# Linear attention into two expert networks on one core: q's softmax subtraction and exponential issued one slot sooner

## Chip, cores and metric

One core of a Trainium2 chip runs the whole kernel. The metric is the device time of one execution in microseconds (us); the median of three runs of the kernel before is 1250.62 us.

## What is computed

The inputs are q, k and v of shape (8 batches, 8 heads, 576 tokens, 64). The reference, cut to what matters:

```python
q_s = softmax(q, axis=-1)            # over the 64 features of a token
k_s = softmax(k, axis=2)             # over the 576 tokens
kv = einsum('bhsd,bhse->bhde', k_s, v)
x = einsum('bhsd,bhde->bhse', q_s, kv)        # then (4608 tokens, 512)
e = argmax(x @ w_gate)               # one of 8 experts per token
y = gate * sigmoid(x @ w_output_gate)[e] * (relu(x @ w1[e]) @ w2[e])
out = max(y @ m1, y @ m2, y @ m3) @ m_out
```

## The kernel before, in words

The kernel has an attention phase that runs beside the experts' matrix products, and then a second network with the products of `m_l1` and `m_l2`. All matrix products of the experts use operands that are split into an upper and a lower part (three products for one), so each product needs two helpers: ScalarE (ACT) writes the upper part, VectorE (DVE) or GpSimd (POOL) the lower part as a difference.

The first phase is written out by hand in **slots**. A slot is one group of 12 expert products (`l1_group`, L604, or `l2_group`, L622), followed by the reading out of its sum from PSUM, and then by the attention steps that were registered for that slot with `at` (L497). `run_events` (L548) issues them in the order in which they were registered; instructions are issued to each engine in exactly this program order, and every engine works its queue in order. A batch has 32 slots, in four blocks of eight groups: `l1`, `l2`, `l1`, `l2`. The `l1` groups and the first block of `l2` are read out by ACT (L616, L634). The second block of `l2` is read out by DVE (L636).

A **unit** is half of a batch's heads, so there are 16 units, n = 0 to 15. Units 0 and 1 run ahead of the experts. Units 2 and 3 have tables of their own (`EARLY`). For n from 4 on the steps stand at `START[n] = 16 n - 51` plus the offsets in `STEADY` (L44): the front steps (`q_max`, `q_exp`, `k_max`, `k_tr`, `k_exp`, `q_sum`, `kv_mm`, `kv_norm`, `kv_lo`, `q_norm`) and, for each of the two pairs of heads, the back steps (`q_tr`, `q_lo`, `x_mm`, `x_lo`, `logit_mm`). One unit starts every 16 slots, so the back steps of the unit before lie beside the front steps of the next one. Around slot START[n] - 2 to START[n] + 1 these are, in the order in which they are registered (steps of unit n-1 come first in a slot):

- slot START - 2: `x_lo` of pair 0 of unit n-1 (DVE, L371); odd slot, so `split_lo` of the experts' weights on POOL (L595)
- slot START - 1: `logit_mm` of pair 0, then `q_tr` of pair 1 of unit n-1 (five transposes on TensorE into PSUM, copied by ACT, L327), then `q_exp` of unit n, then `split_sub` of the experts' weights on ACT (L588)
- slot START: `q_lo` of pair 1 of unit n-1 (DVE, L335, needs the copy of L327), then `k_tr` of unit n (transposes, then DVE L238 and L241)
- slot START + 1: `x_mm` of pair 1 of unit n-1 (six products, L353, need the result of L335), then `k_exp` of unit n (product L248, needs L241; then DVE L251, ACT L253)

`q_exp` (L224) is two instructions on one tile in place: the subtraction of the row maximum on DVE (L228, 128x1280, both inputs in SBUF) and the exponential on ACT (L229). It issues no DMA.

```python
    def q_exp(b, hb):
        u = units[b, hb]
        qt = u["q"].rearrange("p h c d -> p (h c) d")
        eng = nc.gpsimd if (b, hb) == (0, 1) else vec
        eng.tensor_tensor(out=qt, in0=qt, in1=u["qm"].to_broadcast([128, 20, D]), op=ALU.subtract)
        act(out=qt, in_=qt, func=ACTF.Exp)
```

For odd n the slots around START lie in the second block of `l2` (fh = 1, read out by DVE L636), and the router of the batch before still scatters its token table with indirect DMAs from POOL (`route_5`, L489). For even n they lie in the first block of `l2` (fh = 0, read out by ACT L634). On POOL the decoding of the second network's weights also runs there (L685, L686, L695).

Of the kernel before, what the change touches and what calls it, by code (L numbers as in the profile page):

```python
# [16 lines left out]
PSUM = bass.MemoryType.PSUM  # L17
# [11 lines left out]
CAP = 96  # L29
SLOT = 64  # L30
# [4 lines left out]

# batches whose attention output comes from plain float32 products instead of three with split operands
NFULL = 2

# The order of the work beside the experts' matrix products, in slots of one group of 12 products; a unit is
# half of a batch's heads. STEADY: slots after a unit's START for the steps in FRONT, and those in BACK for  # L40
# each pair of heads; EARLY: the same for the first units, from the first slot on. LOAD: a unit's loads.
# ROUTE: the router's steps after START of a batch's second unit, for batch 0 and 1 from the first slot on.
# DEC: pieces of the float64 weights, after START of even units, of odd units and of the last one.
STEADY = ((-4, -1, -4, 0, 1, 3, 6, 6, 7, 8), (10, 10, 13, 14, 15), (15, 16, 17, 18, 19))  # L44
EARLY = {
# [11 lines left out]
def tile_linear_attention__then__moe(  # L57
# [21 lines left out]

# [1 line left out]
    const = ctx.enter_context(tc.tile_pool(name="const", bufs=1))  # L81
# [24 lines left out]

# [1 line left out]
    es_moe = ExitStack()  # L108
# [20 lines left out]

# [1 line left out]
    def setup():  # L131
# [40 lines left out]

# [1 line left out]
    units = {}  # L174
# [197 lines left out]

    # the logits with tokens as columns: column tile c of the array takes tokens 128 c on; the last 64 follow on tile 0
    def logit_mm(b, hb, pr):
# [17 lines left out]

# [1 line left out]
    def route_1(b):  # L394
# [60 lines left out]
    def route_4(b):  # L455
        pool = nc.gpsimd
        r = rt[b]
        oh, cs, nm = r["oh"], r["cs"], r["nm"]
        cb = cbuf[b % 2]
        for c in range(4):  # L460
            pool.tensor_tensor(out=cb[:, c + 1], in0=cb[:, c], in1=cs[:, 0, c], op=ALU.add)
        n_b = n_all[:, E * b:E * b + E]
        s_b = st_all[:, E * b:E * b + E]
        pool.tensor_tensor(out=n_b, in0=r["cnt"], in1=nm[:, 0], op=ALU.mult)
        pool.tensor_copy(pad_a[:, 4:12], n_b)
        pool.tensor_tensor(out=pad_b[:, 4:12], in0=pad_a[:, 4:12], in1=pad_a[:, 3:11], op=ALU.add)
        pool.tensor_tensor(out=pad_a[:, 4:12], in0=pad_b[:, 4:12], in1=pad_b[:, 2:10], op=ALU.add)
        pool.tensor_tensor(out=pad_b[:, 4:12], in0=pad_a[:, 4:12], in1=pad_a[:, 0:8], op=ALU.add)
        pool.tensor_tensor(out=s_b, in0=pad_b[:, 4:12], in1=n_b, op=ALU.subtract)
        pool.tensor_tensor(out=s_b, in0=s_b, in1=base.to_broadcast([128, E]), op=ALU.add)  # L470
        pool.tensor_tensor(out=base, in0=base, in1=pad_b[:, 11:12], op=ALU.add)
        mo = sm.tile([128, 5, E], F32, tag="rmo", name="rmo")
        pool.tensor_tensor(out=mo, in0=oh, in1=nm.to_broadcast([128, 5, E]), op=ALU.mult)
        a = sm.tile([128, 5, E], F32, tag="ra", name="ra")
        pool.tensor_tensor(out=a, in0=cs[:, 1], in1=cb[:, 0:5], op=ALU.add)
        pool.tensor_tensor(
            out=a, in0=a, in1=s_b.rearrange("p (o e) -> p o e", o=1).to_broadcast([128, 5, E]), op=ALU.add
        )
        # the position of a token that leaves its batch's majority expert; BIG for the others
        pool.tensor_scalar(out=a, in0=a, scalar1=-float(BIG), scalar2=None, op0=ALU.add)  # L480
        pool.tensor_tensor(out=a, in0=a, in1=mo, op=ALU.mult)
        for w in (4, 2, 1):
            pool.tensor_tensor(out=a[:, :, 0:w], in0=a[:, :, 0:w], in1=a[:, :, w:2 * w], op=ALU.add)
        pi = sm.tile([128, 5], I32, tag="rpi", name="rpi")
        pool.tensor_scalar(out=pi, in0=a[:, :, 0], scalar1=float(BIG), scalar2=None, op0=ALU.add)
        r["pi"] = pi
# [6 lines left out]

# [1 line left out]
    events = {}  # L495
# [55 lines left out]

# [1 line left out]
    raw_t = {}  # L553
# [98 lines left out]

# [1 line left out]
    dec = deque((i, j) for j in range(8) for i in range(4))  # L654
# [12 lines left out]
    def dec_bits():  # L667
        if not dec_r:
            return
        i, j, raw = dec_r.popleft()  # L670
        lo, hi = raw[:, :, 0], raw[:, :, 1]
        f = dc_p.tile([128, 384], I32, tag="df", name="df")
        p = dc_p.tile([128, 384], I32, tag="dp", name="dp")
        a2 = dc_p.tile([128, 384], F32, tag="da", name="da")
        r = dc_p.tile([128, 384], F32, tag="dr", bufs=2, name="dr")
        # sign, exponent less 896 and the upper 20 bits of the mantissa
        vec.tensor_scalar(out=f, in0=hi, scalar1=0x07FFFFFF, scalar2=3,
                          op0=ALU.bitwise_and, op1=ALU.logical_shift_left)
        vec.scalar_tensor_tensor(out=f, in0=hi, scalar=-0x40000000, in1=f,
                                 op0=ALU.bitwise_and, op1=ALU.bitwise_or)  # L680
        vec.tensor_scalar(out=p, in0=f, scalar1=-0x00800000, scalar2=None, op0=ALU.bitwise_and)
        act(out=a2, in_=hi.bitcast(F32), func=ACTF.Abs)
        # the lower 32 bits, added with one rounding
        act(out=r, in_=lo.bitcast(U32), func=ACTF.Copy, scale=2.0 ** -52)
        nc.gpsimd.tensor_tensor(out=r, in0=r, in1=p.bitcast(F32), op=ALU.mult)  # L685
        nc.gpsimd.tensor_tensor(out=r, in0=r, in1=f.bitcast(F32), op=ALU.add)  # L686
        dec_m.append((i, j, a2, r))

    def dec_store():
        if not dec_m:  # L690
            return
        i, j, a2, r = dec_m.popleft()
        # under float32's range, by the upper word (0x38100000 and on, read as a float): zero
        vec.tensor_scalar(out=a2, in0=a2, scalar1=1.125 * 2.0 ** -15, scalar2=None, op0=ALU.is_ge)
# [9 lines left out]

# [1 line left out]
    m_all = [t.rearrange("p j n -> (p j n)").rearrange("(k f) -> k f", f=F2) for t in w32_d[0:3]]  # L706
# [29 lines left out]

    # ================= program =================
    with tc.manual_schedule():
# [95 lines left out]

# [1 line left out]
        sl = {}  # L836

        def fx_table():
# [43 lines left out]
            vec.tensor_reduce(out=sf[:, 0:4], in_=pr, axis=AX.X, op=ALU.add)  # L882
            # start = valid * (start0 + SLOT * j)
            vec.tensor_scalar(out=sf[:, 4:5], in0=jc, scalar1=float(SLOT), scalar2=None, op0=ALU.mult)
            vec.scalar_tensor_tensor(
                out=sf[:, 2:3], in0=sf[:, 4:5], scalar=sf[:, 3:4], in1=sf[:, 2:3], op0=ALU.mult, op1=ALU.add
            )
            # static start = min(start + CAP * (1 - valid), CAP)
            vec.tensor_scalar(
# [3 lines left out]
            vec.tensor_scalar(out=sf[:, 3:4], in0=sf[:, 4:5], scalar1=float(CAP), scalar2=None, op0=ALU.min)  # L893
            # trips of the general loop: 0 where the static slots cover everything
            nsl = incl[:, w - 1:w]
# [55 lines left out]

        # half a piece of a minority expert's weights: 256 rows of 512 columns
        def fx_w(e_reg, i):
# [33 lines left out]

        # the tokens' upper and lower parts side by side: the first pass multiplies both with the
        # weights' upper part, the second the upper part with the weights' lower part
        def fx_mm(ps, x, ws, kh):  # L990
# [9 lines left out]

        # adds the two parts and turns tokens to columns
        def fx_sum(raw):
# [62 lines left out]

        # steps between the groups of the second network; one that leaves its sum open in PSUM comes
        # only where the next step follows before that bank is needed again
        fix = deque((f, False) for f in (fx_table, fx_gather, fx_soft, lambda: None, fx_tr))
# [12 lines left out]

        # chunks: (sources of y, N, list of (scale, writer))
        def chunk_l2(c, hs, part=0):
# [20 lines left out]

        # chunk B holds the last 64 tokens of each batch, in two parts; the second carries the packed tokens
        order = [(c, 0) for c in range(B)] + [(B, 0), (B, 1)]
# [113 lines left out]
```

## Time and profile before

| what | value |
|---|---|
| runs of the kernel before | 1249.36, 1250.62, 1254.8 us |
| median | 1250.62 us |
| span of the profiled execution | 1248.6 us |
| TensorE busy, share of the span | 1193.2 us, 96% |
| VectorE busy | 647.8 us, 52% |
| ScalarE busy | 447.0 us, 36% |
| GpSimd busy | 380.4 us, 30% |

The page gives the profiled execution's time as its span from the first to the last instruction; no other time of that execution is listed. It is 2.0 us under the median and 0.8 us under the fastest run. Times in the trace count from the span's start. "Busy" leaves out waiting only where the engine had not started an instruction: an instruction that was started and then held up counts as busy for its whole length. PE is TensorE, "idle before" in square brackets is the time that an engine waited for the releaser named.

### The profile page before, as it was taken

The page shows a single profiled execution, that of the slowest core. Times are in us where ns is not written, and L with a number is a line of the kernel's source. Part 1 is how long each engine was busy: PE and PEld are TensorE (multiplying, and loading weights), DVE is VectorE, ACT ScalarE, POOL GpSimd, SP SyncE. Part 2 cuts the span into 40 slices and gives each one's busy share as a digit, 9 for nine tenths or more (in the row PEclk, how much of TensorE's full clock was granted, in tenths as well). Part 3 has the DMA queues.
Part 4 walks back from the last instruction along what each step waited for, and adds up shares of the span by engine and source line. Part 5 has one row for each costly group of instructions (what it writes and reads, how often), then busy time and mean ns, then how long its engine had stood idle before and what let it go on. Part 6 is the DMA issues. An engine that isn't in the chain of part 4 may idle for free. (4 is left out here: it accounts for less than half of the span.)

```text
span 1248.6 us, 19283 instructions
## 1 busy us (share of the span) xinstructions
PE 1193.2 (96%) x7518; PEld 1054.4 (84%) x7518; DVE 647.8 (52%) x1161; ACT 447.0 (36%) x864; POOL 380.4 (30%) x466
## 2 busy tenths in 40 slices
PE   4699999999999999999999999999999999999996
PEld 3598998989899898999888888888888888888995
DVE  7779787787878789534442414132331313232211
ACT  2463554546454554534331223122232213221211
POOL 1257767676776667772002000000000000000000
PEclk9799999999999999999999999999999999999998
DMA  6776555675665544353512121211222111210001
GB/s 167 183 198 175 166 176 159 175 214 148 202 202 164 170 128 148 123 188 99 169 35 79 36 67 52 83 44 34 85 68 76 46 56 51 51 51 1 35 17 24
DMA packets 141455, 135.68 MB, mean 109 GB/s; under 512 B 70045, under 2 KB 104637, under 8 KB 140336
## 3 DMA queue, kind: packets, MB, share of 16 engines
q1 hardware_dynamic: 139648, 134.01, 36.1%
q8 instruction: 61, 1.00, 0.3%
q0 software_dynamic: 1712, 0.39, 0.2%
q14 instruction: 34, 0.28, 0.1%
HBM read 106.99 MB, written 27.62 MB: 108 GB/s over the span
## 5 line engine op out<-in xcount | busy, mean ns | idle before, releaser
L813 PE MATMUL pm<-yh,wf 128*128 128x512 f32 (+2 forms) x2160 | 464.8, 375 | 0.0
L813 PEld LDWEIGHTS pm<-yh,wf 128*128 128x128 f32 x2160 | 385.9, 188 | 72.5
L629 PE MATMUL yp<-h,w 128*128 128x288 f32 x1536 | 226.3, 303 | 0.2 <-DVE h L617 0.2
L611 PE MATMUL hp<-xs,w 128*128 128x288 f32 x1536 | 218.9, 299 | 0.0
L629 PEld LDWEIGHTS yp<-h,w 128*128 128x128 f32 x1536 | 212.1, 192 | 3.6 <-DVE h L617 0.5
L611 PEld LDWEIGHTS hp<-xs,w 128*128 128x128 f32 x1536 | 208.1, 190 | 2.8 <-POOL w L595 0.2
L595 POOL TENSOR_TENSOR w<-stg,w 128x512 fp32r<-128x512 f32 x126 | 179.4, 1427 | 77.0 <-ACT w L588 74.9
L820 DVE TENSOR_TENSOR tm<-tm,pm 128x512 f32<-128x512 f32 (+2 forms) x60 | 38.6, 643 | 256.6 <-ACT tm L819 152.3
L1077 POOL DMA_INDIRECT out_dram<-oc,ftb x1 | 1.0, 983 | 548.4 <-ACTq L1149 548.4
L831 PE MATMUL op<-wo,hc 128*128 128x512 f32 (+1 forms) x666 | 152.8, 390 | 0.0
L831 PEld LDWEIGHTS op<-wo,hc 128*128 128x128 f32 (+1 forms) x666 | 124.5, 187 | 26.3
L819 ACT ACTIVATE tm<-pm 128x512 f32<-128x512 f32 (+2 forms) x60 | 33.7, 562 | 230.9 <-PE pm L813 230.2
L617 DVE SCALAR_TENSOR_TENSOR h<-hp,h 128x288 fp32r<-128x288 f32 x128 | 56.6, 451 | 58.8 <-ACT h L616 58.5
L616 ACT ACTIVATE h<-hp 128x288 fp32r<-128x288 f32 x128 | 52.2, 408 | 84.6 <-PE hp L611 84.2
L588 ACT ACTIVATE w<-stg 128x512 fp32r<-128x512 f32 x128 | 78.8, 621 | 0.0
L823 ACT ACTIVATE hc<-tm 128x512 fp32r<-128x512 f32 (+2 forms) x60 | 35.8, 597 | 93.9 <-DVE tm L821 93.9
L824 DVE TENSOR_TENSOR hc<-tm,hc 128x512 fp32r<-128x512 f32 (+2 forms) x60 | 38.9, 649 | 39.8 <-ACT hc L823 39.8
L833 ACT ACTIVATE oc<-op,tsrc 128x512 f32<-128x512 f32 x32 | 22.1, 689 | 101.9 <-PE op L831 101.9
L489 POOL DMA_INDIRECT tab_d<-tsrc,rpi x40 | 45.9, 1147 | 37.5 <-DMA tab_d<-tsrc,rpi 26.2
L685 POOL TENSOR_TENSOR dr<-dr,dp 128x384 f32<-128x384 f32 x32 | 32.5, 1015 | 53.2 <-ACT h L616 37.3
L228 DVE TENSOR_TENSOR q<-q,qm 128x1280 f32<-128x1280 f32 x15 | 42.7, 2849 | 0.0
L821 DVE TENSOR_TENSOR tm<-tm,pm 128x512 f32<-128x512 f32 (+2 forms) x60 | 38.6, 644 | 7.0 <-DVE tm L820 0.9
(219 smaller groups left out, 1179.1 us busy)
## 6 DMA issues: line engine op xcount, KB each, us to landing
stg<-in_moe_w_dram SPq DMA_DIRECT2D x31, 1024.0 KB, 5.7
fw<-in_moe_w_dram SPq DMA_DIRECT2D x24, 512.0 KB, 3.8
v<-in_v_dram SPq DMA_DIRECT2D x80, 128.0 KB, 4.8
draw<-in_moe_w_dram SPq DMA_DIRECT2D x24, 384.0 KB, 4.1
y_d<-y SPq DMA_DIRECT2D x32, 288.0 KB, 2.7
k<-in_k_dram SPq DMA_DIRECT2D x16, 512.0 KB, 5.2
q<-in_q_dram SPq DMA_DIRECT2D x16, 512.0 KB, 6.6
yr<-y_d SPq DMA_DIRECT2D x8, 1024.0 KB, 5.2
```

Of the source, the lines that this page charges most:

```text
L228: eng.tensor_tensor(out=qt, in0=qt, in1=u["qm"].to_broadcast([128, 20, D]), op=ALU.subtract)
L489: nc.gpsimd.indirect_dma_start(out=tab_d[:, :], out_offset=bass.IndirectOffsetOnAxis(ap=rt[b]["pi"][:, c:c + 1], axis=0), in_=tsrc[:, b, c ...
L588: act(out=t[:, 0], in_=src, func=ACTF.Copy)
L595: eng.tensor_tensor(out=t[:, 1], in0=src, in1=t[:, 0].bitcast(F32), op=ALU.subtract)
L611: mm(ps, w[:, a, kk], xp[b, kk][:, c, cs], start=(n == 0), stop=(n == 11))
L616: act(out=h[:, 0, cs], in_=ps, func=ACTF.Relu)
L617: vec.scalar_tensor_tensor(out=h[:, 1, cs], in0=ps, scalar=0.0, in1=h[:, 0, cs].bitcast(F32), op0=ALU.max, op1=ALU.subtract,)
L629: mm(ps, w[:, a, f], ht[f][:, c, cs], start=(n == 0), stop=(n == 11))
L813: mm(pp[m][:, 0:n], wf[f][:, a, m, kk], ys[kk][:, c, 0:n], start=(kk == 0 and i == 0), stop=(kk == 3 and i == 2))
L820: vec.tensor_tensor(out=tv, in0=tv, in1=pp[1][:, 0:n], op=ALU.max)
L824: vec.tensor_tensor(out=h[:, 1, 0:n], in0=tv, in1=h[:, 0, 0:n].bitcast(F32), op=ALU.subtract)
L831: mm(ps[0:m], hs[f][:, a, 128 * t:128 * t + m], wo[f][:, c], start=(i == 0), stop=(i == 17))
```

## The change

In every unit from n = 4 on, `q_exp` is registered for slot START - 2 instead of START - 1. No instruction is added or removed. In that slot it comes behind `x_lo` of pair 0 of unit n-1, and ahead of the next slot's read-out and of `q_tr` of pair 1. The rest of the diff removes comment lines.

```diff
-STEADY = ((-4, -1, -4, 0, 1, 3, 6, 6, 7, 8), (10, 10, 13, 14, 15), (15, 16, 17, 18, 19))
+STEADY = ((-4, -2, -4, 0, 1, 3, 6, 6, 7, 8), (10, 10, 13, 14, 15), (15, 16, 17, 18, 19))
```

## Rows read from the trace of the kernel before

**Rows 1.** Part 1 of the page: busy time, share and instructions of each engine.

```profile
PE 1193.2 (96%) x7518; PEld 1054.4 (84%) x7518; DVE 647.8 (52%) x1161; ACT 447.0 (36%) x864; POOL 380.4 (30%) x466
```

**Rows 2.** Waits of TensorE: line, releaser, us in total, times, longest.

```profile
PE xT L353 <- DVE qTs L335: 14.2, 6, 2.7
PE kB L248 <- DVE dg L241: 13.1, 9, 8.0
```

**Rows 3.** Timeline around unit 7 (odd): start, us, engine, line, tiles [idle before].

```profile
189.51 0.82 DVE L371 TENSOR_TENSOR xs<-xr,xs 128x576 fp32r<-128x576 f32 x1
189.88 1.39 POOL L489 DMA_INDIRECT tab_d<-tsrc,rpi  x1 [0.17 <-issue]
...
190.24 0.65 ACT L327 ACTIVATE qTs<-qT 128x576 fp32r<-128x576 f32 x1 [2.53 <-PE qT L321]
190.26 0.45 DVE L636 TENSOR_TENSOR y<-yp,y 128x288 f32<-128x288 f32 x1
190.63 4.30 DVE L228 TENSOR_TENSOR q<-q,qm 128x1280 f32<-128x1280 f32 x1
191.31 1.30 POOL L595 TENSOR_TENSOR w<-stg,w 128x512 fp32r<-128x512 f32 x1
...
192.55 1.02 POOL L695 TENSOR_TENSOR dr<-da,dr 128x384 f32<-128x384 f32 x1
...
194.96 1.27 ACT L229 ACTIVATE q<-q 128x1280 f32<-128x1280 f32 x1 [4.07 <-DVE q L228]
195.22 0.74 DVE L335 TENSOR_TENSOR qTs<-qT,qTs 128x576 fp32r<-128x576 f32 x1
...
196.02 1.05 PE L353 MATMUL xT<-qTs,kvs 128*128 128x288 f32 x6 [2.22 <-DVE qTs L335]
...
197.56 0.67 PE L248 MATMUL kB<-dg,ones 128*128 128x256 f32 x2 [0.49 <-DVE dg L241]
```

**Rows 4.** Windows: length, busy of PE, PEld, DVE, ACT, POOL, PEclk, DMA share, GB/s.

```profile
193.80:198.20 4.40, 1.69 (x9) 1.44 (x10) 3.95 (x7) 2.85 (x4) 2.79 (x2) 1.00 0.83 256
198.20:201.70 3.50, 3.50 (x17) 3.50 (x16) 2.17 (x3) 2.06 (x3) 2.29 (x2) 0.51 0.07 20
...
478.70:482.00 3.30, 2.81 (x18) 2.55 (x19) 2.77 (x5) 2.08 (x4) 1.12 (x1) 1.00 0.57 196
```

**Rows 5.** Timeline around unit 6 (even).

```profile
155.64 0.41 ACT L634 ACTIVATE y<-yp 128x288 f32<-128x288 f32 x1 [0.80 <-PE yp L629]
...
155.95 0.75 DVE L371 TENSOR_TENSOR xs<-xr,xs 128x576 fp32r<-128x576 f32 x1
...
156.17 1.40 POOL L695 TENSOR_TENSOR dr<-da,dr 128x384 f32<-128x384 f32 x1 [0.54 <-DVE da L694]
...
156.62 2.30 DVE L228 TENSOR_TENSOR q<-q,qm 128x1280 f32<-128x1280 f32 x1
...
158.84 0.74 DVE L335 TENSOR_TENSOR qTs<-qT,qTs 128x576 fp32r<-128x576 f32 x1
158.95 1.28 ACT L229 ACTIVATE q<-q 128x1280 f32<-128x1280 f32 x1 [1.42 <-DVE q L228]
...
160.27 0.96 PE L353 MATMUL xT<-qTs,kvs 128*128 128x288 f32 x6
...
161.06 0.59 PE L248 MATMUL kB<-dg,ones 128*128 128x256 f32 x2
```

**Rows 6.** Timeline around unit 10 (even).

```profile
296.87 2.81 POOL L695 TENSOR_TENSOR dr<-da,dr 128x384 f32<-128x384 f32 x1 [0.56 <-DVE da L694]
...
297.31 1.50 DVE L228 TENSOR_TENSOR q<-q,qm 128x1280 f32<-128x1280 f32 x1
```

**Rows 7.** Timeline near 74 us: two L371 in a row beside L489.

```profile
73.92 2.17 DVE L371 TENSOR_TENSOR xs<-xr,xs 128x576 fp32r<-128x576 f32 x2
74.97 1.44 POOL L489 DMA_INDIRECT tab_d<-tsrc,rpi  x1 [0.18 <-PE kv L286]
75.34 0.75 DVE L371 TENSOR_TENSOR xs<-xr,xs 128x576 fp32r<-128x576 f32 x1
```

## The prediction

> **What bounds the kernel now.** I read the page's busy times first. TensorE is busy for 96% of the span [rows 1], so time is gained or lost almost only where TensorE stands still, or where its clock falls. The waits of TensorE say where it stands still. Two of them touch the change [rows 2]: the products L353 of `x_mm` wait 14.2 us in all for DVE's L335, six times, and the product L248 of `k_exp` waits 13.1 us for L241, of which 8.0 us is one wait at the start of the kernel. Then I read the timeline around slot START of each unit. The six waits for L335 lie at the six odd units 5 to 15; rows 3 show unit 7, the others look alike. The even units 6 to 14 have none; rows 5 show unit 6. Unit 4 has an `EARLY` unit before it and nothing waits there. Last, the windows show what follows such a wait [rows 4]: TensorE is busy 1.69 of 4.40 us, and in the next 3.50 us its granted clock is 0.51, that is its lower level, 1.2 GHz. Such a stretch follows the wait in five of the six odd units. In the sixth it does not come (the window at 478.70 has a clock of 1.00).
>
> **Why L335 is late in odd units.** The subtraction L228 starts at 190.63 and is on record for 4.30 us [rows 3]. In unit 10 it takes 1.50 us [rows 6]. So 2.8 us of it is waiting, while three POOL instructions run: L489 to 191.27, L595 to 192.61, L695 to 193.57; 194.93 less 1.48 is 193.45, just when L695 ends. L335 stands behind it on DVE and starts at 195.22, and TensorE has waited 2.22 us. In the even unit the subtraction is held up by 0.8 us only, by one L695 [rows 5].
>
> **The change, part by part.** Two instructions move, no DMA moves, and no queue of SP or POOL is passed. On TensorE nothing moves.
>
> *On DVE, odd units.* The subtraction passes one instruction, the read-out L636 of 0.45 us, and stands right behind L371. By itself that moves only 0.37 us (190.63 to 190.26). What matters is who holds POOL off: now the subtraction asks while L489 already runs; then it asks at the end of L371, which keeps L489 waiting (1.39 us on record). The trace does not show this pair, so I bound it. At one end nothing changes and the subtraction ends at 194.93. At the other it follows L371 at once and ends at 190.26 + 1.50 = 191.76. Two rows lie near the second end. Near 74 us two L371 follow each other, L489 asks 0.37 us before the second starts, and that second one takes 0.75 us, not longer than an undisturbed one [rows 7]; in the odd units L489 asks 0.38 us before. In unit 10, L695 asks 0.44 us before the subtraction, which takes 1.50 us all the same [rows 6]. Against it stand four of the five even units, where an L695 that asked 0.45 us before gets in first [rows 5]. The row with the same POOL instruction is that of rows 7, so I take 191.76.
>
> *On ACT, all units.* The exponential now stands **ahead** of `q_tr`'s copy L327, and of the read-out of slot START - 1 where ACT does it. Before, L327 ran at 190.24 while DVE was still subtracting. Now L327, and L335 which needs it, wait for subtraction plus exponential.
>
> *Odd unit, sum.* Exponential 191.79 to 193.06 (1.27), L327 to 193.7 (0.65), L335 to about 194.45 (0.74), against 195.96 before: 1.5 us sooner, so TensorE's wait falls from 2.2 to 0.7 us. Six units give -9.0 us. L248 now waits up to 0.50 us more; it can lose that or gain as much, and I take -1 us over the six. The low clock costs about half of 3.5 us, 1.7 us [rows 4]; a wait of 0.7 us is too far from the 2.2 to bring it, so five times 1.7 go: -8.5 us. Together -18.5 us.
>
> *Even unit, sum.* Here L636 is not on DVE, so the order on DVE stays the same and the subtraction still ends at 158.92 [rows 5]. The cover that kept `q_tr`'s copy free is gone. ACT then runs the exponential to 160.23, L634 (0.41) to 160.55 and L327 (0.65) to 161.15 (one starts some 0.09 us before the other's end), and L335 runs to 161.9, against 159.58. L353, which started at 160.27 without a wait, starts at about 161.95. In the odd unit 1.60 us lie between the end of L335 and the start of L248 (195.96 to 197.56); so L248 starts at 163.5 instead of 161.06. That is +2.4 us on TensorE, four times, +9.6 us; unit 10, whose subtraction is 0.8 us shorter, I put at +1.1. The clock may now fall here: two waits of 1.7 and some 0.7 us, a little under the 2.7 us of the odd units, of which five in six fell. I take two of five, +3.4 us; the ends are 0 and +8.5. Together +14.1 us, and nothing is behind it that could take it up, since TensorE is the bound before and after.
>
> *Later steps.* `q_sum` and what follows it stand three slots later and wait for nothing that q's exponential gives, so an earlier result is worth nothing there. The weights' copy L588 behind `q_tr` is up to 0.9 us later in even units; its weights are for slots eight later, so this is covered.
>
> Sum: -18.5 + 14.1 = -4.4 us. The span is 1248.6 us, 2.0 us under the median of the runs; set on the median of 1250.6 this gives 1246.2 us.
>
> **Rivals.**
>
> *POOL keeps its place (slower).* The subtraction again waits for L489, L595 and L695 and ends at 194.93. Then exponential and copy come on top: L327 to 196.8, L335 to 197.6 instead of 195.96, +1.6 us in six units, +9.8. The sixth odd unit may get the low clock too, +1.7. With the even units' +14.1 that is +25.6 us: 1276 us. It decides at the moment when L371 ends: if L489 gets in before the subtraction. For it: the four even units. Against it: rows 7.
>
> *The subtraction comes in right behind L489.* It would run from 191.27 to 192.75, 1.0 us later than I take it. L335 then ends at about 195.45, 0.5 us sooner than now, -3 us over six units; the total wait is near 2 us, so perhaps three of five low clocks go, -5.1. Net +6.0 us: 1257 us. For it: in rows 5 the subtraction runs when one POOL instruction ends, though L595 is next in the queue. Against it: in rows 3 it let two more go first. The Trainium skill, "SBUF — State Buffer", section "Who interferes with whom", says that a VectorE instruction with two SBUF inputs and a GpSimd one that reads SBUF exclude each other, and that whichever issues first holds the port for its whole length. By that rule, with L489 issued first, this rival's time would come. Rows 5 agree (0.8 us late, the rest of L695); rows 3 do not, as L595 and L695 were issued after the subtraction and still ran before it.
>
> *The even units lose nothing (faster).* Should the copy L327 not be held up there, only the odd units' gain remains: -18.5 us, 1232 us. It would need another order on ACT than the registration gives, so this is also the case that the change doesn't do what it says.
>
> **How the numbers follow.** My case has 0.66, POOL keeping its place 0.16, the place behind L489 0.13, no loss in even units 0.05. Within my case the clock in even units (0 to +8.5) and L248 in odd units (-2 to +2) give 1240 to 1253. The range takes in this case, the second rival and the nearer edge of the first: 1236 to 1270. A measurement of this kernel can tell some 0.5%, 6.25 us, from no change. Faster by more than that is 0.4 of my case and all of the last: 0.31. Slower is the first rival, half of the second and a little of mine: 0.25. Within 0.5% is left with 0.44.
>
> **What would show it.** In the changed profile: L228 near 1.5 us in odd units (4.3 if POOL kept its place, 2.5 behind L489); L327 right after L229 on ACT in every unit; the wait of L353 for L335 below 1 us in odd units and a new one of 1.5 to 2 us in even units, so about 11 waits instead of six; low-clock stretches gone in odd units and some in even ones. Wrong would be an L353 without waits in even units, or low clocks in most of them.

## The result, and the profile after

The changed kernel takes 1258.89 us (median of four runs, 1257.13 to 1260.01) against 1250.22 us for the kernel before in the same series: a ratio of 1.0065, 95% interval 1.0046 to 1.0083. It is slower by 0.65%. The prediction was 1246.2 us, faster by 4.4 us; the measured time lies in its range (1236 to 1270), on the side to which it gave 0.25.

The span of the profiled execution went from 1248.6 to 1258.2 us. The waits of TensorE show at once that there are now eleven waits for L335 instead of six, shorter ones, and that the time has come up at L248 [rows 2]. Waits of TensorE in the changed kernel:

```profile
PE kB L248 <- DVE dg L241: 20.6, 13, 8.0
PE xT L353 <- DVE qTs L335: 12.5, 11, 1.9
```

**Even units.** Around unit 6 of the kernel before, the copy L327 ran while DVE was still at the subtraction (a row of the same stretch as [rows 5]):

```profile
156.88 0.65 ACT L327 ACTIVATE qTs<-qT 128x576 fp32r<-128x576 f32 x1 [0.83 <-PE qT L321]
```

Timeline around unit 6 of the changed kernel:

```profile
156.68 0.75 DVE L371 TENSOR_TENSOR xs<-xr,xs 128x576 fp32r<-128x576 f32 x1
...
157.35 2.31 DVE L228 TENSOR_TENSOR q<-q,qm 128x1280 f32<-128x1280 f32 x1
...
159.69 1.27 ACT L229 ACTIVATE q<-q 128x1280 f32<-128x1280 f32 x1 [4.11 <-DVE q L228]
160.87 0.39 ACT L634 ACTIVATE y<-yp 128x288 f32<-128x288 f32 x1
161.16 0.64 ACT L327 ACTIVATE qTs<-qT 128x576 fp32r<-128x576 f32 x1
...
161.83 0.76 DVE L335 TENSOR_TENSOR qTs<-qT,qTs 128x576 fp32r<-128x576 f32 x1 [2.18 <-ACT qTs L327]
...
162.65 1.06 PE L353 MATMUL xT<-qTs,kvs 128*128 128x288 f32 x6 [1.86 <-DVE qTs L335]
...
164.10 0.69 PE L248 MATMUL kB<-dg,ones 128*128 128x256 f32 x2 [0.40 <-DVE dg L241]
```

The subtraction stands as before, right behind L371, and takes 2.31 us (2.30). ACT sits idle for 4.11 us in front of the exponential, and only then comes the copy L327; DVE idles 2.18 us for it, TensorE 1.86 us and another 0.40 us.

**Odd units.** Three more rows around unit 7 of the kernel before, behind those of [rows 3]:

```profile
194.31 1.50 POOL L489 DMA_INDIRECT tab_d<-tsrc,rpi  x1 [0.74 <-DMA tab_d<-tsrc,rpi]
195.84 1.29 POOL L595 TENSOR_TENSOR w<-stg,w 128x512 fp32r<-128x512 f32 x1
196.33 1.09 DVE L241 TENSOR_SCALAR dg<-ident,m 128x128 f32<-128x128 f32 x2
```

The same stretch of the changed kernel:

```profile
194.24 0.83 DVE L371 TENSOR_TENSOR xs<-xr,xs 128x576 fp32r<-128x576 f32 x1
194.62 1.40 POOL L489 DMA_INDIRECT tab_d<-tsrc,rpi  x1 [0.16 <-issue]
195.00 1.48 DVE L228 TENSOR_TENSOR q<-q,qm 128x1280 f32<-128x1280 f32 x1
196.05 1.59 POOL L595 TENSOR_TENSOR w<-stg,w 128x512 fp32r<-128x512 f32 x1
...
196.51 1.27 ACT L229 ACTIVATE q<-q 128x1280 f32<-128x1280 f32 x1 [4.17 <-DVE q L228]
...
197.69 0.64 ACT L327 ACTIVATE qTs<-qT 128x576 fp32r<-128x576 f32 x1
...
198.36 0.76 DVE L335 TENSOR_TENSOR qTs<-qT,qTs 128x576 fp32r<-128x576 f32 x1 [1.15 <-ACT qTs L327]
...
199.09 1.00 POOL L489 DMA_INDIRECT tab_d<-tsrc,rpi  x1 [0.48 <-DMA tab_d<-tsrc,rpi]
...
199.17 1.05 PE L353 MATMUL xT<-qTs,kvs 128*128 128x288 f32 x6 [0.74 <-DVE qTs L335]
199.48 2.20 DVE L241 TENSOR_SCALAR dg<-ident,m 128x128 f32<-128x128 f32 x2
200.12 1.27 POOL L595 TENSOR_TENSOR w<-stg,w 128x512 fp32r<-128x512 f32 x1
...
201.83 0.86 PE L248 MATMUL kB<-dg,ones 128*128 128x256 f32 x2 [1.60 <-DVE dg L241]
```

The subtraction now runs at once behind L371 and takes 1.48 us instead of 4.30, and the wait at L353 is 0.74 us instead of 2.22. L489 beside it lasts 1.40 us, as it did before (1.39) when the subtraction came later, so its row doesn't show it waiting for the subtraction; L595 behind it lasts 1.59 us instead of 1.30. But 0.4 us after the end of L335 the two small L241 instructions meet the next L489 and then L595, and the first of them is held until L595 is over: the two take 2.20 us, before 1.09. L248 waits 1.60 us, before 0.49. The two waits together are 2.34 us (2.71 before), and the clock still falls behind them. Windows of the changed kernel (columns as in [rows 4]):

```profile
196.40:201.90 5.50, 3.16 (x23) 2.72 (x21) 4.32 (x8) 3.66 (x5) 4.49 (x4) 1.00 0.77 243
201.90:205.60 3.70, 3.70 (x15) 3.59 (x16) 1.64 (x2) 1.35 (x2) 1.69 (x2) 0.54 0.38 143
...
164.60:168.00 3.40, 3.40 (x16) 3.38 (x15) 2.16 (x2) 2.15 (x3) 0.00 (x0) 0.50 0.03 6
```

Such stretches follow four of the six odd units and one even unit (the last line, unit 6): five in all, as before.

To say where the time went I took, from the start times of TensorE's instructions, the length of the stretch from 80 products ahead of a unit's first L248 to 90 behind it. It holds the same 170 products in every kernel here. Summed over the six odd units (5 to 15) and the five even ones (6 to 14), in us, with the low-clock stretches between 100 and 540 us:

```
kernel                              odd units   even units   low clock
before                                145.6        102.2      5
changed                               141.0        115.2      5
e3  subtraction alone moved           119.6        108.1      0
e4  order on ACT alone changed        157.9        110.5      6 (four of them twice as long)
e1  odd units alone                   136.1        105.3      2
e2  even units alone                  147.4        117.9      9
e5  changed, L241 on ACT              127.0        120.6      5
e6  subtraction alone, L241 on ACT    119.6        109.3      1
e7  changed, no scatter               144.2        116.1      8
e8  before, no scatter                132.3        102.2      0
e9  best version                      120.5        102.7      0
e10 odd units alone, L241 on ACT      126.9        107.3      0
e11 before, L241 on ACT               147.7        106.2      6
```

Each row is read from one profiled execution; those of e5 and e9 took 2.6 and 2.4 us more than the median of their runs. In the changed kernel the odd units gained 4.6 us and the even ones lost 13.0 us; with 0.3 us at unit 4 that leaves +8.7 of the +9.6 us between the two spans.

### The profile page after: what moved, and what is told of

Its sections match the earlier page's. It is cut to its first block, busy times and chain, and to the rows that moved or that the text cites. A ratio compares the mean times of both kernels' runs of the same rounds, so it can differ in the third digit from the quotient of the medians.

```text
span 1258.2 us, 19283 instructions
## 1 busy us (share of the span) xinstructions
PE 1196.4 (95%) x7518; PEld 1055.0 (84%) x7518; DVE 642.3 (51%) x1161; ACT 445.4 (35%) x864; POOL 381.7 (30%) x466
## 5 line engine op out<-in xcount | busy, mean ns | idle before, releaser
L595 POOL TENSOR_TENSOR w<-stg,w 128x512 fp32r<-128x512 f32 x126 | 179.9, 1432 | 90.3 <-ACT w L588 88.5
L617 DVE SCALAR_TENSOR_TENSOR h<-hp,h 128x288 fp32r<-128x288 f32 x128 | 56.6, 451 | 58.4 <-ACT h L616 58.0
L489 POOL DMA_INDIRECT tab_d<-tsrc,rpi x40 | 45.1, 1126 | 36.4 <-DMA tab_d<-tsrc,rpi 24.9
L695 POOL TENSOR_TENSOR dr<-da,dr 128x384 f32<-128x384 f32 x32 | 37.7, 1179 | 13.5 <-DVE da L694 13.5
```

The lines of the kernel that those rows point to most:

```text
L489: nc.gpsimd.indirect_dma_start(out=tab_d[:, :], out_offset=bass.IndirectOffsetOnAxis(ap=rt[b]["pi"][:, c:c + 1], axis=0), in_=tsrc[:, b, c ...
L595: eng.tensor_tensor(out=t[:, 1], in0=src, in1=t[:, 0].bitcast(F32), op=ALU.subtract)
L617: vec.scalar_tensor_tensor(out=h[:, 1, cs], in0=ps, scalar=0.0, in1=h[:, 0, cs].bitcast(F32), op0=ALU.max, op1=ALU.subtract,)
```

## Experiments

Two theories stood against each other. A: the change is two changes that can be taken apart, the subtraction's place on DVE (a gain in odd units) and the exponential's place ahead of L327 on ACT (a loss in all). B: the subtraction's earlier place costs by itself.

**The subtraction alone.** `STEADY` is that of the change, but the exponential becomes a step of its own that stays in slot START - 1 (the lines of the edit that matter, from three places):

```diff
+    q_pow = lambda b, hb: (lambda t: act(out=t, in_=t, func=ACTF.Exp))(units[b, hb]["q"].rearrange("p h c d -> p (h c) d"))
-        act(out=qt, in_=qt, func=ACTF.Exp)
+        q_pow(b, hb) if 2 * b + hb < 4 else None
-        for d, f in zip(t[0], FRONT):
+        for d, f in zip(t[0] + (-1,) * (n > 3), FRONT + (q_pow,)):
```

> Only the subtraction moves to slot START - 2; the exponential stays in START - 1 behind q_tr's copy L327, so the order on ACT is that of the kernel before and the order on DVE that of the changed one. Theory A (two separate orders: the subtraction's place on DVE gains in odd units, the exponential's place ahead of L327 on ACT costs in all): L228 is 1.5 us in odd units, L327 runs as before, L353 waits for L335 less than 1 us in all (14.2 before, 12.5 in the changed kernel), even units are as before; 14 us of waits and up to five low-clock stretches of 1.7 us go, L248 may wait up to 1.7 us more in each odd unit: 1226 to 1240 us. Theory B (the subtraction's earlier place on DVE costs by itself, by what it pushes back there): as slow as the changed kernel, 1255 to 1262 us.

Measured: 1241.63 us, ratio 0.9929 (0.9904 to 0.9954). That is 1.6 us outside the range of theory A and 13 us away from that of B. Around unit 7 (the exponential has line 173 here):

```profile
190.01 0.66 ACT L327 ACTIVATE qTs<-qT 128x576 fp32r<-128x576 f32 x1 [2.53 <-PE qT L321]
190.12 1.48 DVE L228 TENSOR_TENSOR q<-q,qm 128x1280 f32<-128x1280 f32 x1
...
191.63 1.28 ACT L173 ACTIVATE q<-q 128x1280 f32<-128x1280 f32 x1 [0.96 <-DVE q L228]
192.25 0.74 DVE L335 TENSOR_TENSOR qTs<-qT,qTs 128x576 fp32r<-128x576 f32 x1
...
193.41 0.96 PE L353 MATMUL xT<-qTs,kvs 128*128 128x288 f32 x6
```

L327 is done before the subtraction ends, L353 waits for nothing in odd units, no clock falls between 100 and 540 us, and the odd units are 26 us shorter. Only 9 us of that reach the end, and its waits of TensorE name most of the rest:

```profile
PE kB L248 <- DVE dg L241: 15.1, 6, 8.0
PE qT L320 <- DVE qn L268: 9.1, 7, 2.7
...
PE xT L353 <- DVE qTs L335: 0.5, 2, 0.3
```

In the kernel before, L320 waited once:

```profile
PE qT L320 <- DVE qn L268: 2.7, 1, 2.7
```

Now it waits for q's division L268 after each odd unit (6.4 us more): behind unit 7 TensorE is ready for it 17.6 us after L248 instead of 19.0, while L268 lasts 2.21 us instead of 1.48. And the even units are 6 us longer: three of them now wait 1.5 to 1.8 us for L241, though nothing of theirs moved on ACT. In just these three (6, 8 and 12) the subtraction went ahead of POOL's L695, which waits for it (2.81 us), and POOL's next instructions then meet L241; around unit 6:

```profile
155.25 2.81 POOL L695 TENSOR_TENSOR dr<-da,dr 128x384 f32<-128x384 f32 x1 [0.53 <-DVE da L694]
155.68 1.50 DVE L228 TENSOR_TENSOR q<-q,qm 128x1280 f32<-128x1280 f32 x1
...
158.01 2.52 POOL L595 TENSOR_TENSOR w<-stg,w 128x512 fp32r<-128x512 f32 x2
158.21 2.41 DVE L241 TENSOR_SCALAR dg<-ident,m 128x128 f32<-128x128 f32 x2
```

In units 10 and 14 the subtraction waits for L695 (2.31 us), and L248 does not wait.

**The order on ACT alone.** Subtraction and exponential stay in slot START - 1, but are registered ahead of the steps of unit n-1, so DVE's order is that of before and ACT's that of the change:

```diff
-            at(LOAD.get(n, START.get(n - 2, 0) + 9), load_unit, b, hb)
+            at(LOAD.get(n, START.get(n - 2, 0) + 9), load_unit, b, hb); n == 15 or at(START[n + 1] - 1, q_exp, *divmod(n + 1, 2))
-            if d is not None:
+            if d is not None and (f is not q_exp or n < 4):
```

> Subtraction and exponential stay in slot START - 1, but are issued ahead of the steps of the unit before in that slot: the order on DVE is that of the kernel before, the exponential stands ahead of L327 on ACT. Theory A: L228 stays at 4.3 us in odd units, L335 comes 1.6 us later there (+10 us, and a sixth low clock), even units lose some 2 us each as in the changed kernel (+10 us): 1265 to 1282 us. Theory B: the order on ACT does not matter, 1247 to 1254 us.

Measured: 1272.38 us, ratio 1.0174 (1.0148 to 1.0199): theory A. Rows around unit 7:

```profile
194.37 4.31 DVE L228 TENSOR_TENSOR q<-q,qm 128x1280 f32<-128x1280 f32 x1
...
198.71 1.27 ACT L229 ACTIVATE q<-q 128x1280 f32<-128x1280 f32 x1 [7.35 <-DVE q L228]
...
199.89 0.63 ACT L327 ACTIVATE qTs<-qT 128x576 fp32r<-128x576 f32 x1
```

The subtraction keeps its 4.31 us, ACT idles for 7.35 us, and the copy comes after both. L353 waits 28.4 us in eleven waits. This is also what the prediction's first rival (POOL keeps its place) would have looked like; it gave 1276 us for it.

**Odd units alone, even units alone.** `MOVED` is the changed `STEADY`:

```diff
-            t = STEADY
+            t = MOVED if n % 2 == 1 else STEADY
```

> The change in odd units 5 to 15 only. In the two profiles the odd units together took 4.5 us less with the change, the even ones 13 us more. Theory A: only the odd units' part is left, 1242 to 1249 us, with four or five low-clock stretches still there and L248 waiting some 1.6 us in odd units. Theory B: each unit that is moved costs, 1251 to 1257 us.

> The change in even units 4 to 14 only. Theory A: the odd units stay as before (L228 at 4.3 us, five or six waits for L335 of 2.3 us), the even ones lose 13 us: 1259 to 1267 us. Theory B: half of the changed kernel's loss, 1252 to 1256 us.

Measured: odd units alone 1247.62 us, ratio 0.9969 (0.9951 to 0.9986); even units alone (n % 2 == 0) 1266.34 us, ratio 1.0114 (1.0094 to 1.0134). Both as theory A has it. The odd units' low clocks were fewer than expected, two instead of four or five; the even units brought more, three, and 15.7 us in their stretches.

**Is it L241 that takes the odd units' gain?** Theory C says yes, theory D that L248 is late for another reason. L241 goes to ACT:

```diff
-            vec.tensor_scalar(
-                out=u["dg"][:, i], in0=ident, scalar1=m2[:, i:i + 1], scalar2=None, op0=ALU.mult
+            act(
+                out=u["dg"][:, i], in_=ident, func=ACTF.Copy, scale=m2[:, i:i + 1]
```

> The changed kernel, with the two L241 instructions (the diagonal of the maxima) issued on ACT instead of DVE in every unit. Theory C (in odd units the changed kernel's gain is taken back by L241, a DVE instruction of 0.3 us that is held for 2.0 to 2.2 us while POOL runs L489 and then L595): on ACT it takes some 0.3 us each, the waits of L248 in odd units fall from 1.6 us to under 0.4, and most of the four low-clock stretches in odd units go; even units keep their wait for L335: 1242 to 1250 us. Theory D (L248 is late because DVE's queue is late there, L241 itself does not matter; or ACT has no room): 1255 to 1262 us.

Measured: 1257.02 us, ratio 1.0035 (1.0017 to 1.0054). Theory C's time was missed by 7 us and theory D's came, though each of theory C's signs in odd units is there. Around unit 7:

```profile
198.00 1.07 PE L353 MATMUL xT<-qTs,kvs 128*128 128x288 f32 x6 [0.74 <-DVE qTs L335]
198.31 0.70 ACT L241 ACTIVATE dg<-ident,m 128x128 f32<-128x128 f32 x2 [0.64 <-DVE m L238]
...
199.06 0.70 PE L248 MATMUL kB<-dg,ones 128*128 128x256 f32 x2
```

L248 no longer waits, no odd unit has a low clock, and their stretches fall from 141.0 to 127.0 us. But the even units rose to 120.6: four of the five low clocks come with their waits at L353, the fifth (at 220.0 us) behind a wait of 1.50 us at L320 for L268. In unit 6 the wait at L353 is now 2.51 us instead of 1.86:

```profile
150.70 0.96 PE L353 MATMUL xT<-qTs,kvs 128*128 128x288 f32 x6
...
156.88 2.32 DVE L228 TENSOR_TENSOR q<-q,qm 128x1280 f32<-128x1280 f32 x1
...
162.19 1.81 PE L353 MATMUL xT<-qTs,kvs 128*128 128x288 f32 x6 [2.51 <-DVE qTs L335]
```

TensorE reaches pair 0 of that unit at 150.70, in the changed kernel at 151.81: 1.1 us sooner. The subtraction comes only 0.5 us sooner (156.88, 157.35): what DVE and ACT do ahead of it got no shorter. So part of what TensorE saves in an odd unit it waits out in the next even one. To take the even units out of the question I put L241 on ACT without their move, and without any move:

> The change in odd units only (1247.6 us as it stood), with L241 on ACT in every unit. Theory C (L241, held by POOL, takes the odd units' gain back): the stretch around START of the six odd units falls to some 21.1 us as in the changed kernel with L241 on ACT, 9 us less in all, and L248's waits of 1.8 us in two even units go: 1234 to 1241 us. Theory F (what L241 on ACT saves is given back by other waits, as it was in the changed kernel, 1257.0 against 1258.9 us): 1244 us and more.

> The kernel before with L241 on ACT, nothing moved. There the exponential and the weights' copy L588 stand ahead of L241 on ACT, and L241 is ready as early on DVE: L248 waits about as before in odd units (0.5 us each) and some 0.5 to 1 us in even ones. Theories C and F both: 1248 to 1256 us; anything under 1244 us would say that L241 on DVE already cost time before the change.

Measured: 1246.08 us, ratio 0.9962 (0.9948 to 0.9976), and 1256.08 us, ratio 1.0040 (1.0024 to 1.0056), on one chip. Theory C's sign is there (126.9 us in the odd units, 21.1 each), but its time was missed again. L241 on ACT costs 5 us by itself in the kernel before: there it stands behind the exponential, and L248 waits for it in every unit from 5 on (17.4 us in 14 waits, one of 8.1 us at the start of the kernel; before 13.1 us), with a sixth low clock. Against its own control, moving the odd units gains 10.0 us (1256.08 to 1246.08); with L241 on DVE it gained 3.3 us (1250.92 to 1247.62). The difference of 6.7 us is the most that L241 held on DVE takes back of the odd units' gain. About 2 us of it may come from the control: with nothing moved, L241 on ACT made the odd units 2.1 us longer (147.7 against 145.6), and the move takes that away too. Theory F's number came true; its reason, that nothing is saved, did not.

**Which POOL instructions hold DVE?** The scatter L489 of batches 1 to 7 is left out, in the changed kernel and in the kernel before:

```diff
-            for c in range(5):
+            for c in range(0):
                 at(r2 + 5 + 2 * c, route_5, b, c)
```

> The changed kernel without the router's scatter L489 of batches 1 to 7: those tokens that leave their batch's majority expert get no second treatment, so these rows of the output are left as the majority expert gives them. Theory C: with no L489 ahead of it, L241 is held by one L595 at most (under 1.3 us), L248 waits under 0.6 us in odd units, low-clock stretches there mostly go: 1243 to 1251 us. Theory E (any POOL instruction that is running holds L241 for about 2 us): waits of 1.5 us and more stay in odd units, 1255 us and more.

> The kernel before without the scatter L489 of batches 1 to 7 (the same rows of the output are left out). Theory C: a DVE instruction that asks while L489 runs lets POOL's following instructions go first; without L489 the subtraction of odd units waits for one POOL instruction at most: L228 1.5 to 2.4 us instead of 4.3, the six waits of 2.3 us for L335 fall under 0.6 us, the low-clock stretches go: 1226 to 1238 us. Theory E: L228 still waits for L595 and L695, 3.8 us and more, 1246 to 1254 us.

Measured: the kernel before without it 1232.31 us, ratio 0.9846 (0.9821 to 0.9872), inside theory C's range: L228 took 2.21 us in odd units instead of 4.30, and no clock fell. Around the same unit 7:

```profile
187.80 1.80 POOL L595 TENSOR_TENSOR w<-stg,w 128x512 fp32r<-128x512 f32 x1
...
188.75 2.21 DVE L228 TENSOR_TENSOR q<-q,qm 128x1280 f32<-128x1280 f32 x1
189.57 2.27 POOL L695 TENSOR_TENSOR dr<-da,dr 128x384 f32<-128x384 f32 x1
...
192.35 2.04 DVE L241 TENSOR_SCALAR dg<-ident,m 128x128 f32<-128x128 f32 x2
```

The subtraction waits for the one L595 that runs, and L695 then waits for the subtraction (2.27 us instead of 1.02). But L241 is held here too, for 2.04 us beside two L595, with no L489 near: for L241 the scatter is not needed. In the changed kernel without the scatter, 1257.09 us, ratio 1.0046 (1.0032 to 1.0060), missed theory C's time: L241 fell to 1.0 us as it said, but L595 moved up in POOL's queue and the subtraction took 2.57 us instead of 1.48, so L353 waits 18.4 us in all, and there are eight low clocks, one at each of the six odd units.

**A faster version.** First the subtraction alone with L241 on ACT, then in addition the exponential in slot START, behind L241 (offset 0 instead of -1 for `q_pow`):

> The kernel with only the subtraction moved (1241.6 us), with L241 on ACT as well. Theory C: the waits of L248 in its even units (1.5 to 1.8 us, three or four times) go, the rest stays: 1233 to 1239 us. Theory D: nothing changes, 1239 to 1244 us; or ACT, which now stands behind the exponential there, makes L241 later: 1245 us and more.

> As the kernel with only the subtraction moved and L241 on ACT (1242.6 us), but the exponential comes in slot START behind the two L241, so it no longer stands ahead of them on ACT. If what is left at L248 (eight waits, 16.1 us in all, 8.1 of them at the start) is the exponential ahead of L241 on ACT, the waits in the five even units fall from 1.0 us each to under 0.4 and the low-clock stretch there goes: 1234 to 1239 us. If ACT is simply full there, the read-outs L634 and L361 behind the later exponential come late instead and TensorE waits for those: 1241 us and more.

Measured: 1242.55 us, ratio 0.9926 (0.9903 to 0.9949), no better than the subtraction alone, so theory C's time was missed there: L248 now waits for ACT's L241 instead, 0.65 to 0.97 us in each of the five even units. And with the exponential later 1237.56 us, ratio 0.9897 (0.9880 to 0.9914), as expected and 1.0% faster than the kernel before; L248 waits at the start of the kernel only. Whether it is faster than the subtraction alone (0.9929) stays open, as the two intervals overlap. On ACT around unit 6 of the last one:

```profile
155.55 0.66 ACT L327 ACTIVATE qTs<-qT 128x576 fp32r<-128x576 f32 x1 [0.66 <-PE qT L321]
...
158.83 0.70 ACT L241 ACTIVATE dg<-ident,m 128x128 f32<-128x128 f32 x2 [1.07 <-DVE m L238]
159.43 1.26 ACT L173 ACTIVATE q<-q 128x1280 f32<-128x1280 f32 x1
```

The exponential, which nothing needs for three more slots, stands behind the two instructions that TensorE needs first, L327 and L241. Beside the waits at the start of the kernel, what is left is 7.7 us for L268 and 6.3 us for L617.

## Why the prediction was wrong

- *Even units, +14.1 us:* right. Measured +13.0 us in their stretches; L335 ended at 162.59 - 157.35 = 5.2 us after the subtraction's start, predicted 5.3 (161.9 - 156.62). One low clock instead of the two it counted on; the unit with the short subtraction was not 10, but 8 and 14.
- *The subtraction follows L371 at once:* right. 1.48 us in all six odd units. The row that decided (two L371 in a row) was the right one to go by. The second rival (right behind L489) did not come; that its 1257 us lie nearest to the measured time is chance.
- *What holds the subtraction, told by how long before it POOL asked:* not borne out. Over all runs, L695 was issued 0.22 to 0.25 us after the start of the L371 ahead of the subtraction, and went first 39 times and second 26 times in that same stretch of times. What the six odd units share with the row that decided is L489, which lasts 1.40 us beside the subtraction in all of them.
- *L353 in odd units falls to 0.7 us:* right, 0.73 to 0.74 us in five of them, 1.04 in unit 5.
- *"L248 now waits up to 0.50 us more; it can lose that or gain as much, and I take -1 us over the six":* **this step failed.** The waits of L248 in the odd units grew from 2.3 us in all to 8.3 us (1.69, 1.60, 1.74, 1.58, none, 1.65). The step kept L241 as long as in the rows of before, where L489 was over when it came and only one L595 ran beside it (1.09 us for the two, 0.6 us of it held), and did not ask what POOL would be running at the new time of L241. In unit 7 it asks while L489 still runs, and L595, issued later, goes first, as it did with the subtraction before.
- *"a wait of 0.7 us is too far from the 2.2 to bring it, so five times 1.7 go: -8.5 us":* failed with it. By itself 0.7 us does not bring the low clock: in e5 and e10, where 0.7 to 1.0 us at L353 are all that is left, it follows in none of twelve odd units. But with L248's wait added, five of the six odd units still waited 2.3 to 2.7 us in all (2.3 to 3.2 before; unit 13 waited 0.74), and four of the six still had the low clock: -1.7 us instead of -8.5.

The two failed terms are worth 7 us (+6.0 instead of -1) and 6.8 us; put in, the odd units' -18.5 us becomes -4.7 us (measured -4.6), and the sum +9.4 us with the predicted even units. That in the changed kernel the low clock of odd units needs L241's part of the wait is shown by e5 and e10. It needs no hold of L241 in general: in e7 L241 takes 1.0 us, and all six odd units have the low clock behind 1.82 to 2.18 us at L353 and up to 0.4 us at L248. The span "1240 to 1253" of the prediction's own case follows from its terms only if set on the profiled span; set on the median, as its sum is, it is 1242 to 1254. Nothing hangs on that.

The Trainium skill, "SBUF — State Buffer", section "Who interferes with whom", lists `tensor_scalar` among the VectorE operations that can take the port pair shared with GpSimd. L241 agrees (two of them 0.48 us when undisturbed, 2.20 us beside POOL). The same section of the Trainium skill says that the issue order decides who blocks. Here L241 issued at 199.48, L595 at 200.12, and L595 went first, so on that point the rows differ, as they did for the subtraction before; and in the changed kernel the subtraction ran for 1.48 us although L489 was issued 0.38 us ahead of it and still running.

Not settled: why a DVE instruction that asks while POOL runs is let in at the end of that instruction in some rows (unit 6) and only after one or two more in others (unit 7 before, L241 after). The scatter makes the long case for the subtraction (e8), but L241 was held without it. Not settled either is why waits of one size are followed by the low clock or not: 0.74 and 1.58 us in unit 11 of the changed kernel were not, 0.74 and 1.60 us in unit 7 were.

## What to carry to other kernels

A step that is issued sooner moves on every engine's queue at once; look at each queue for what now stands behind it, and move only the instruction that gains (here the subtraction, while the exponential was better off later). Time saved at one wait is kept only if the next thing that the bounding engine needs is also ready sooner: follow the chain past the wait that goes, to the next two or three. Where two engines hold each other off, cost an instruction at its new time by what the other engine runs then, not by its length in the old place.

## What was not expected of the hardware

Small DVE instructions can be held for several times their own length: one L241 of 128x128, 0.28 us when free, lasted 2.0 us beside POOL's L489 and L595. Two waits of 0.74 and 1.60 us, with products between them, were followed by the lower clock just as one wait of 2.2 us was; the pair 1.74 and 0.42 us in unit 10 of the changed kernel was not, nor 0.74 and 1.58 us in unit 11.
